# The first steps of a convolution kernel in another order: two transforms interleaved, eleven input blocks held, one product folded into the sum

## The chip, the cores and the metric

The kernel runs on one core of a Trainium2 chip. The metric is the device time of one execution in microseconds (us). Before the change it is 835.12 us, the median of three runs (835.08, 835.12 and 838.7).

The engines are named as the profile names them: PE (TensorE, matmuls), PEld (its weight loads), DVE (VectorE), ACT (ScalarE), POOL (GpSimd), and SP, whose queue starts nearly all DMAs.

## The reference

```python
def _attn_ref(x, h):                     # x (8, 6336, 128), h (6336, 128)
    L = 2 * S
    Xf = np.fft.rfft(x, n=L, axis=1)
    Hf = np.fft.rfft(h, n=L, axis=0)
    return np.fft.irfft(Xf * Hf[None, :, :], n=L, axis=1)[:, :S, :]

def _moe_ref(x, w_gate, w1, w2, capacity):        # capacity 128, on the result above
    scores = np.einsum('bsd,d->bs', x, w_gate)
    out = x.copy()
    for b in range(B):
        top_idx = np.argpartition(-scores[b], capacity)[:capacity]
        xe = x[b, top_idx]
        ye = np.maximum(xe @ w1, 0.0) @ w2
        g = 1.0 / (1.0 + np.exp(-scores[b, top_idx]))
        out[b, top_idx] = x[b, top_idx] + g[:, None] * ye
    return out
```

A causal convolution of every batch with h over 6336 positions, done by transforms, and then an expert on the 128 best rows of each batch. Everything is float32.

## The kernel before, in words

The length is split as 50 x 128 (n1 by n2), so a transform has two steps of matmuls. Eight units of work carry the input x (units 0 to 7); unit -1 is h itself. Steps of a unit:

- **a**: the products over n1. A unit has eight input blocks (q = 0 to 7) of 512 KB. A block is loaded (`load_x`, L112 to L117), folded by a sum and a difference of its halves (`fold`, L119 to L122, 128x512 each), and multiplied in two steps t = 0, 1 of 16 matmuls (`products_a`, L166 to L181; the trace shows 32 matmuls a step). The results leave PSUM by copies (`leave_a`, L183 to L197).
- **h**: the products of h over n2, in 13 chunks of four k (the last has two), `stage_h` L214 to L244: matmuls into a ring of four PSUM banks, two turned products on ACT and the cosine product in place (L229, L230), then `join` on DVE, which adds the two (L237) and has the spectrum written twice to DRAM as `hd` (L241).
- **b**: the products of a unit of x over n2, 13 chunks, `stage_b` L246 to L273: matmuls (L251), two products with the spectrum on DVE (L268, one in place in `reg` or `big`, one into a buffer `tx`), and a sum and a difference of them on POOL (L273). `tx` and `st` come from one ring of five buffers (`wide`). The matrix of a chunk (`tab_wb`) and its spectrum are loaded to the six slots of `wbuf`.
- **c**, **d**: back over n2 and n1 (L286, L303), and then the scores, the search for the best rows and the experts. The change does not touch them.

A list named `plan` holds all steps in program order; each engine and SP's queue runs its instructions in that order, and `merge` (L633) interleaves two lists evenly. For the first steps the list is: all of a(-1), all of a(0), then 13 steps "j", then all of a(1). Step j of chunk c has the h products of chunk c+1 and the b products of unit 0 of chunk c, with the spectrum taken from SBUF. From then on c of a unit is merged with b of the next, and a with d. Six blocks are held at first; the load of a later block waits until the block whose slot it takes has been used. Of the folds those of blocks 0 to 15, 21 and 23 are DVE's, the others POOL's.

Of the kernel before, what the change touches and what calls it, by code (L numbers as in the profile page):

```python
# [33 lines left out]
def conv_moe(ctx, tc, x, h, w_gate, w1, w2, fa_d, wb_d, wc_d, at_d, tri_d, cst_d, out):  # L34
# [26 lines left out]
    hring = banks + [spare]  # L61

# [41 lines left out]
    def place(n):  # L104
# [4 lines left out]
        i = 10 + max(0, q - 4) % 3 if u >= 2 else 3 + n % 6 if n < 16 else n - 13  # L109
# [104 lines left out]
    def stage_h(c, wt):  # L214
# [6 lines left out]
        for k in range(0, kn, 2):  # L221
            pt = turn(hring)
            for i in range(2):
                nc.tensor.matmul(pt[:, i * 256:i * 256 + 256], wt[:, k + i], rows_of(-1, k0 + k + i),  # L224
                                 start=True, stop=True)
            pv = pt.rearrange("p (a r d) -> p a r d", r=2, d=HD)
            tv = turned[:, k * 256:k * 256 + 512].rearrange("p (a r d) -> p a r d", r=2, d=HD)
# [415 lines left out]
    plan = merge(a_list(-1), a_list(0)[:0]) + merge(a_list(0), [])  # L643
    plan += [("j", -1, c) for c in range(len(KCH))] + merge(a_list(1), [])
# [13 lines left out]
    users = [s for s in plan if s[0] in "bdj"]  # L658
# [6 lines left out]
    def ask(used):  # L665
        while asked[0] < len(users):
# [4 lines left out]
            if sum(1 if o[0] == "j" else 0 if o in own else 3 if o[0] == "b" and o[1] >= SINGLE else 2  # L671
# [23 lines left out]
    for n in range(6):  # L695
        load_x(n)
# [18 lines left out]
    for s in plan:  # L715
        kind, unit = s[0], s[1]
        n = (unit + 1) * 8
        if kind in "bdj":
            ask(used)
            used += 1  # L720
        if kind == "a":
            q, t = s[2:]
            if unit < 2 and t == 0:
                fold_to(min(n + q + 4, 15) if unit < 1 else 23)
# [7 lines left out]
            if t and n + q < 10:  # L732
                load_x(n + q + 6)
# [179 lines left out]
```

## Time and profile before

| | us |
|---|---|
| median of three runs | 835.12 |
| the profiled execution | 838.41 |
| its span in the trace | 836.6 |
| PE busy | 756.0 (90%) |
| DVE busy | 653.6 (78%) |
| POOL busy | 547.3 (65%) |
| ACT busy | 383.6 (46%) |
| chain that ended last: PE 69%, DVE 19%, issue 6%, DMA 4% | |

The profiled execution took 1.8 us more than its span, and 3.3 us more than the median of the runs. Busy time is an average over stages with different limits, so the first stages have to be read apart. The granted clock of TensorE is given as a share of full speed: 1.00 is 2.4 GHz, 0.50 is 1.2 GHz.

### The profile page before, as it was taken

What the parts mean: (1) busy time and instruction counts of PE and PEld (TensorE: products, weight loads), DVE (VectorE), ACT (ScalarE), POOL (GpSimd) and SP (SyncE); (2) the same over time, 40 slices, a digit from 0 to 9 for tenths busy, and PEclk for the clock granted to TensorE, in tenths of its full rate; (3) what the DMA queues carried; (4) which work ended last, traced back from release to release, by engine and by line L of the source; (5) the groups of instructions that cost most, each with busy time, mean ns of one, the idle gap of its engine ahead of it and who ended that gap; (6) DMA issues with size and microseconds to landing.
All of it is one profiled execution on the core that took longest, in us unless ns stands there. A gap on an engine that the chain in (4) does not pass through costs nothing.

```text
span 836.6 us, 36709 instructions
## 1 busy us (share of the span) xinstructions
PE 756.0 (90%) x16189; PEld 676.5 (81%) x16189; DVE 653.6 (78%) x1103; ACT 383.6 (46%) x625; POOL 547.3 (65%) x387
## 2 busy tenths in 40 slices
PE   6699899999999999999999999899999997689733
PEld 6688788898889888898888888788897887578733
DVE  6459846756576798999778998899689989876882
ACT  5587543464346334543464346433653343233340
POOL 0029929966987699679866896569865566125531
PEclk9899899999999999999999999999999999889966
DMA  8639536468737864777377646796678455204400
GB/s 296 212 133 346 171 121 221 146 213 251 272 109 230 260 228 125 229 246 257 107 228 246 209 151 199 252 322 206 202 232 256 132 165 174 83 10 133 136 11 9
DMA packets 82135, 157.45 MB, mean 188 GB/s; under 512 B 9350, under 2 KB 30072, under 8 KB 81976
## 3 DMA queue, kind: packets, MB, share of 16 engines
q1 hardware_dynamic: 81080, 154.05, 57.1%
q8 instruction: 127, 2.08, 1.0%
q0 software_dynamic: 896, 1.05, 0.5%
q14 instruction: 32, 0.26, 0.1%
HBM read 121.77 MB, written 33.29 MB: 185 GB/s over the span
## 4 chain that ended last, share of the span: by engine, by line
PE 69%; DVE 19%; issue 6%; DMA 4%; POOL 1%; SPq 0%; ACT 0%; POOLq 0%; DVEq 0%; ACTq 0%
PE pb L286 23%; PE pt L251 18%; PE pb L303 11%; PE pt L180 10%; DVE cmp L418 3%; PE pb L180 2%; PE pb L570 2%; DVE num L420 2%; DVE tx L268 2%; DMA out<-st 1%; DVE ss L319 1%; PE pb L224 1%; DVE reg L262 1%; DMA big<-tab_wb 1%; DVE st L307 1%
## 5 line engine op out<-in xcount | busy, mean ns | idle before, releaser
L287 ACT COPY half<-pb 114x512 f32<-114x512 f32 x224 | 147.3, 658 | 248.2 <-PE pb L286 247.4
L314 POOL TENSOR_TENSOR tm<-st,wg 114x1024 f32<-114x1024 f32 x63 | 151.0, 2399 | 80.3 <-DVE st L308 49.5
L273 POOL TENSOR_TENSOR big<-big,tx 128x512 f32<-128x512 f32 (+1 forms) x104 | 131.5, 1297 | 77.2 <-DVE tx L268 65.3
L273 POOL TENSOR_TENSOR reg<-reg,tx 128x512 f32<-128x512 f32 (+1 forms) x104 | 130.7, 1290 | 53.4 <-DVE tx L268 29.7
L286 PEld LDWEIGHTS pb<-wc,reg 128*50 128x50 f32 x4096 | 121.0, 129 | 12.2 <-issue 8.9
L286 PEld LDWEIGHTS pb<-wc,big 128*50 128x50 f32 x4096 | 118.3, 127 | 14.8 <-issue 13.2
L286 PE MATMUL pb<-wc,reg 128*50 128x64 f32 x4096 | 125.8, 223 | 1.4 <-DVE st L308 1.4
L286 PE MATMUL pb<-wc,big 128*50 128x64 f32 x4096 | 122.6, 221 | 0.0
L303 PE MATMUL pb<-half,wbuf 114*50 114x128 f32 x1792 | 110.4, 273 | 7.3 <-DVE st L308 5.1
L303 PEld LDWEIGHTS pb<-half,wbuf 114*50 114x50 f32 x1792 | 95.7, 122 | 17.5 <-DVE st L308 5.9
L251 PE MATMUL pt<-big,wbuf 128*128 128x256 f32 x352 | 88.0, 396 | 0.0
L251 PE MATMUL pt<-reg,wbuf 128*128 128x256 f32 x352 | 87.7, 397 | 0.0
L307 DVE TENSOR_TENSOR st<-pb,st 114x512 f32<-114x512 f32 x64 | 44.1, 688 | 55.6 <-PE pb L303 42.1
L268 DVE TENSOR_TENSOR tx<-pt,wbuf 128x1024 f32<-128x1024 f32 (+1 forms) x65 | 76.3, 1174 | 0.0
L251 PEld LDWEIGHTS pt<-big,wbuf 128*128 128x128 f32 x352 | 64.4, 188 | 14.4 <-DVE tx L268 0.5
L251 PEld LDWEIGHTS pt<-reg,wbuf 128*128 128x128 f32 x352 | 63.9, 188 | 14.0
L197 ACT COPY reg<-pt 128x800 f32<-128x800 f32 x66 | 58.0, 929 | 33.8 <-PE pt L180 32.2
L268 DVE TENSOR_TENSOR reg<-pt,wbuf 128x1024 f32<-128x1024 f32 (+1 forms) x39 | 45.9, 1177 | 24.3 <-PE pt L251 24.3
L197 ACT COPY big<-pt 128x800 f32<-128x800 f32 x59 | 51.6, 929 | 22.9 <-PE pt L180 22.9
L322 DVE TENSOR_REDUCE ss<-tm 114x16 f32<-114x1024 f32 x48 | 58.4, 1216 | 2.3 <-POOL tm L314 1.7
L180 PE MATMUL pt<-fa,big 50*64 50x100 f32 x2336 | 59.1, 249 | 0.2 <-issue 0.2
L180 PEld LDWEIGHTS pt<-fa,big 50*64 50x64 f32 x2336 | 51.8, 133 | 6.3 <-issue 3.7
(159 smaller groups left out, 1118.1 us busy)
## 6 DMA issues: line engine op xcount, KB each, us to landing
wbuf<-tab_at SPq DMA_DIRECT2D x128, 200.0 KB
out<-st SPq DMA_DIRECT2D x128, 200.0 KB
wbuf<-tab_wb SPq DMA_DIRECT2D x84, 256.0 KB
wbuf<-hd SPq DMA_DIRECT2D x84, 256.0 KB
big<-in_x SPq DMA_DIRECT2D x37, 512.0 KB
half<-in_x SPq DMA_DIRECT2D x15, 512.0 KB
hd<-st SPq DMA_DIRECT2D x24, 256.0 KB
reg<-in_x SPq DMA_DIRECT2D x12, 512.0 KB
```

The costliest lines, as they stand in the source:

```text
L180: nc.tensor.matmul(o, w, tab[lanes, c], start=True, stop=True)
L197: nc.scalar.copy(out=o, in_=i)
L251: nc.tensor.matmul(pt[:, k * 256:k * 256 + 256], wt[:, k], rows_of(unit, k0 + k), start=True, stop=True)
L268: v.tensor_tensor(out=dst.rearrange("p h a j k t -> p k h a j t"), in0=src, in1=w, op=ALU.mult)
L273: g.tensor_tensor(out=yv[:, :, r], in0=yv[:, :, r], in1=zv[:, :, 1 - r], op=ALU.add if r else ALU.subtract)
L286: nc.tensor.matmul(pt[i2 * 64:i2 * 64 + N1, o:o + HD], w, wc[:, i2], start=True, stop=True)
L287: nc.scalar.copy(out=hv[0:LN, c * 4 + j:c * 4 + j + 2].rearrange("p j r m t -> p (j r) t m"), in_=pt[0:LN].rearrange("p (j t m) -> p j t m ...
L303: nc.tensor.matmul(pt[r][a * 64:a * 64 + N1, c * 128:c * 128 + 128], ats[c // 2][0:LN, c % 2, a, r], hv[0:LN, :, r, m], start=True, stop=True)
L307: v.tensor_tensor(out=st[:, 0:512], in0=pt[1][0:LN], in1=st[:, 512:1024], op=ALU.add)
L314: e.tensor_tensor(out=tm.rearrange("p (a d) -> p a d", d=n), in0=st.rearrange("p (a d) -> p a d", d=n), in1=w.unsqueeze(1).broadcast_to([L ...
L322: v.tensor_reduce(out=ss[u][:, :, :, 4 * i:4 * i + 4].rearrange("p b s c -> p s c b"), in_=tm.rearrange("p (s c b d) -> p s c b d", s=2, c ...
L418: v.tensor_tensor(out=cv, in0=cur.unsqueeze(2).broadcast_to([LN, nb, nv, HD]), in1=nth[:, :, 0:nv].unsqueeze(3).broadcast_to([LN, nb, nv, ...
```

## The change

The list of first steps becomes: all of a(-1); the 13 h steps merged with all of a(0); the 13 b steps of unit 0 merged with the first five blocks of a(1); the last three blocks of a(1). With it:

- the step "j" is gone. Unit 0 now gets its matrix and its spectrum by `load_b` as the later units do, so `tab_wb` is loaded a second time and `hd` is read back for it; a join is put one chunk after its h step.
- eleven blocks are held (slots 2 to 12) in place of six, and eight blocks of h and three of x are asked for before the first step.
- POOL folds blocks 9, 11, 13, 15 and 16 to 23; DVE folds 0 to 8, 10, 12 and 14.
- the results of a(0) leave by ACT for t = 0 and by DVE for t = 1; five half banks of a(-1) leave by DVE; a(1) uses four single banks (`fringe`) and leaves by ACT.
- ACT no longer multiplies by the cosine: `join` does it in one SCALAR_TENSOR_TENSOR with the sum.

```diff
+    fringe = [(banks[0], banks[1], None), (banks[2], spare, None)]
...
-        i = 10 + max(0, q - 4) % 3 if u >= 2 else 3 + n % 6 if n < 16 else n - 13
+        i = 10 + max(0, q - 4) % 3 if u >= 2 else 2 + n % 11
...
-        if unit < 2:
+        if unit == -1:
             pt = turn(wheel)
+        elif unit == 1:
+            pt = turn(fringe)
...
-        if unit == 1 and q > 2:
-            engines = "sv" if pt[2] is None else "v" if pt[2] is pairs[0] else "s"
+        if unit == -1 and pt[2] is None and q % 3:
+            engines = "sv"
+        if unit == 0 and t:
+            engines = "v"
...
-            nc.scalar.mul(out=pt, in_=pt, mul=cst[:, 2:3])
...
-                v.tensor_tensor(out=sv[:, k:k + 2], in0=got[k // 2].rearrange("p (k a d) -> p k a d", a=4, d=HD),
+                v.scalar_tensor_tensor(out=sv[:, :, k:k + 2], in0=got[k // 2].rearrange("p (a k d) -> p a k d", a=4, d=HD),
+                                       scalar=cst[:, 2:3], op0=ALU.mult, op1=ALU.add,
...
-    plan = merge(a_list(-1), a_list(0)[:0]) + merge(a_list(0), [])
-    plan += [("j", -1, c) for c in range(len(KCH))] + merge(a_list(1), [])
+    chunks = range(len(KCH))
+    plan = merge(a_list(-1), []) + merge([[("h", -1, c)] for c in chunks], a_list(0))
+    plan += merge([[("b", 0, c)] for c in chunks], a_list(1)[0:5]) + merge(a_list(1)[5:], [])
...
-    for n in range(6):
+    for n in range(8):
+        load_x(n)
+    nc.sync.dma_start(out=cst, in_=cst_d)
+    nc.sync.dma_start(out=fa, in_=fa_d[:, 0])
+    for n in range(8, 11):
         load_x(n)
...
-            fold(done[0], v if done[0] < 16 or done[0] in (21, 23) else g)
+            fold(done[0], v if done[0] < 8 or done[0] < 16 and done[0] % 2 == 0 else g)
...
-                fold_to(min(n + q + 4, 15) if unit < 1 else 23)
+                fold_to(min(n + q + 4, 23))
...
-            if t and n + q < 10:
-                load_x(n + q + 6)
+            if t and n + q < 13:
+                load_x(n + q + 11)
...
+        elif kind == "h":
+            spectra.append(stage_h(s[2], tabs.pop(s)[0]))
+            if s[2]:
+                spectra.pop(0)()
+        elif kind == "b":
+            if spectra:
+                spectra.pop(0)()
```

PE after the first unit, before: the last step of a(0) (L180, two banks of `pt`), and then h (L224) and b (L251) by turns.

```order
L180 MATMUL pt_69<-fa,half 64x2x50 x16
L224 MATMUL pb_70<-reg_75,wbuf 128x256 x2
L224 MATMUL pb_71<-reg_75,wbuf 128x256 x2
L224 MATMUL pb_72<-reg_75,wbuf 128x256 x2
L224 MATMUL pm<-reg_75,wbuf 128x256 x2
L251 MATMUL pt_68<-big,wbuf 128x256 x4
```

PE at the same stage now (L183 is a, L229 is h):

```order
L229 MATMUL pb_72<-reg_75,wbuf 128x4x64 x2
L229 MATMUL pm<-reg_75,wbuf 128x4x64 x2
L183 MATMUL pt_68<-fa,big 64x2x50 x16
L183 MATMUL pt_69<-fa,big 64x2x50 x16
L229 MATMUL pb_70<-reg_75,wbuf 128x4x64 x2
L229 MATMUL pb_71<-reg_75,wbuf 128x4x64 x2
```

The steps of a(0) now stand between h chunks, and no b stands there.

DVE in a(-1), before, from the fold of block 6 on, with the waits (L121 and L122 are the two halves of a fold):

```order
L121 TENSOR_TENSOR half<-half 128x512 [waits DMAHW7_49,PE_49]
L122 TENSOR_TENSOR half<-half 128x8x64 [waits DVE_49,PE_49]
L121 TENSOR_TENSOR half<-half 128x512 [waits DMAHW0_49,PE_49]
L122 TENSOR_TENSOR half<-half 128x8x64 [waits DVE_49,PE_49]
L121 TENSOR_TENSOR half<-half 128x512 [waits DMAHW1_49,PE_49]
```

DVE now, from the fold of block 7 on (L122 and L123 are the fold, L198 the copy of a half bank, `big` holds the first blocks of x):

```order
L122 TENSOR_TENSOR half<-half 128x512
L123 TENSOR_TENSOR half<-half 128x8x64
L122 TENSOR_TENSOR big<-big 128x512
L123 TENSOR_TENSOR big<-big 128x8x64
L198 COPY reg_75<-pb_71 128x2x200 x2
L122 TENSOR_TENSOR big<-big 128x512
L123 TENSOR_TENSOR big<-big 128x8x64
L198 COPY reg_75<-pb_71 128x2x200
```

Copies that PE's ring of PSUM buffers waits for now stand behind folds that do not wait for PE.

POOL from its first b chunk on, before (L273 is b, L121 and L122 a fold):

```order
L273 TENSOR_TENSOR big<-big,tx 128x2x32x8 x6
L121 TENSOR_TENSOR half<-half 128x512
L122 TENSOR_TENSOR half<-half 128x8x64
L273 TENSOR_TENSOR big<-big,tx 128x2x32x8 x4
L121 TENSOR_TENSOR half<-half 128x512
```

POOL now, from the fold of block 19 and the first b chunk on (L276 is b):

```order
L122 TENSOR_TENSOR big<-big 128x512
L123 TENSOR_TENSOR big<-big 128x8x64
L276 TENSOR_TENSOR big<-big,tx 128x2x32x8 x2
L122 TENSOR_TENSOR big<-big 128x512
L123 TENSOR_TENSOR big<-big 128x8x64
L276 TENSOR_TENSOR big<-big,tx 128x2x32x8 x4
L122 TENSOR_TENSOR big<-big 128x512
```

Between the first and the last of its 13 b chunks POOL has four folds, both before (blocks 16 to 19) and now (20 to 23); eight others stand ahead of the first chunk now.

## Rows read from the trace of the kernel before

**Rows 1.** Stages; columns: window, us, busy (instructions) by engine, PEclk, DMA share, GB/s
```profile
0.00:24.20 24.20, 15.22 (x525) 14.38 (x528) 15.19 (x24) 13.81 (x21) 0.20 (x4) 1.00 0.87 292
24.20:46.03 21.83, 16.82 (x509) 16.11 (x500) 6.50 (x10) 13.84 (x22) 0.00 (x0) 0.77 0.48 163
46.03:95.66 49.63, 46.51 (x203) 37.10 (x200) 44.13 (x52) 37.33 (x77) 37.91 (x31) 1.00 0.75 261
95.66:112.96 17.30, 15.53 (x512) 14.82 (x513) 11.10 (x12) 9.80 (x15) 10.08 (x8) 0.80 0.11 38
112.96:836.60 723.64, 661.91 (x14454) 594.07 (x14453) 576.70 (x1006) 308.81 (x492) 499.12 (x345) 0.97 0.58 184
```

**Rows 2.** Chain of waits, pieces in order of time: start us, us, what
```profile
20.72 2.31 issue
23.43 1.37 PE pt L180 x64
...
36.38 2.52 issue
...
57.26 1.82 PE pt L251 x8
59.07 1.83 PE pb L224 x8
```

**Rows 3.** DVE, timeline: start us, us, engine, line, op [idle before]
```profile
5.10 0.69 DVE L121 TENSOR_TENSOR half<-half 128x512 f32<-128x512 f32 x1 [4.10 <-DMA half<-in_h]
...
6.44 0.69 DVE L121 TENSOR_TENSOR half<-half 128x512 f32<-128x512 f32 x1
```

**Rows 4.** DVE, groups by line: busy us, mean ns | idle before
```profile
L237 DVE TENSOR_TENSOR st<-pb,half 128x512 f32<-128x512 f32 x19 | 12.5, 682 | 13.7 <-ACT pb L230 13.7
L195 DVE COPY reg<-pt 128x800 f32<-128x800 f32 x3 | 3.0, 993 | 0.3
L195 DVE COPY reg<-pb 128x400 f32<-128x400 f32 x4 | 2.3, 576 | 5.9 <-PE pb L180 5.9
L485 DVE SCALAR_TENSOR_TENSOR work<-pm,work 114x256 bf16<-114x256 f32 x6 | 2.3, 418 | 0.1
```

**Rows 5.** Timeline where DVE and POOL fold together
```profile
99.90 1.72 POOL L121 TENSOR_TENSOR half<-half 128x512 f32<-128x512 f32 x1
...
100.52 1.65 DVE L122 TENSOR_TENSOR big<-big 128x512 f32<-128x512 f32 x1
```

**Rows 6.** DVE, timeline: the two products of the first b chunk
```profile
51.80 1.23 DVE L268 TENSOR_TENSOR big<-pt,st 128x1024 f32<-128x1024 f32 x1 [0.84 <-PE pt L251]
52.95 1.21 DVE L268 TENSOR_TENSOR tx<-pt,st 128x1024 f32<-128x1024 f32 x1
```

**Rows 7.** POOL, timeline: its first b chunk, a fold, two later chunks
```profile
54.34 2.50 POOL L273 TENSOR_TENSOR big<-big,tx 128x512 f32<-128x512 f32 x2 [53.89 <-DVE tx L268]
...
64.09 1.28 POOL L121 TENSOR_TENSOR half<-half 128x512 f32<-128x512 f32 x1
...
66.69 4.98 POOL L273 TENSOR_TENSOR big<-big,tx 128x512 f32<-128x512 f32 x4
```

**Rows 8.** Issues of DMAs up to 114 us: count, KB each
```profile
half<-in_h SPq DMA_DIRECT2D x8, 512.0 KB
hd<-st SPq DMA_DIRECT2D x24, 256.0 KB
wbuf<-tab_wb SPq DMA_DIRECT2D x15, 256.0 KB
```

**Rows 9.** Two stretches with the DMA engines full, columns as in rows 1
```profile
5.00:12.00 7.00, 6.01 (x146) 5.71 (x150) 6.72 (x11) 2.80 (x5) 0.00 (x0) 1.00 1.01 373
60.00:80.00 20.00, 19.97 (x87) 16.10 (x87) 19.58 (x25) 15.95 (x33) 18.56 (x16) 1.00 0.98 343
```

**Rows 10.** PE, timeline: the first matmuls of a(1), with the wait ahead of them
```profile
95.66 1.01 PE L180 MATMUL pb<-fa,half 50*64 50x100 f32 x32 [3.07 <-DVE st L237]
```

**Rows 11.** The stretch from there on, columns as in rows 1
```profile
95.66:104.00 8.34, 7.96 (x208) 7.77 (x212) 6.38 (x6) 4.61 (x8) 8.26 (x7) 0.59 0.22 75
```

More of the change, by code (lines that the diff above doesn't have):

```diff
@@ L223, in stage_h @@
             for i in range(2):
[L224 to L227, printed above, removed]
+                nc.tensor.matmul(pt.rearrange("p (a i j t) -> p i a j t", i=2, j=32, t=2)[:, i], wt[:, k + i],
+                                 rows_of(-1, k0 + k + i).rearrange("p (a j) t -> p a j t", a=4), start=True, stop=True)
+            pv = pt.rearrange("p (u r x) -> p u r x", r=2, u=2)
+            tv = turned[:, k * 256:k * 256 + 512].rearrange("p (u r x) -> p u r x", r=2, u=2)
             for r in range(2):
                 nc.scalar.mul(out=tv[:, :, 1 - r], in_=pv[:, :, r], mul=cst[:, 3 + r:4 + r])
-            nc.scalar.mul(out=pt, in_=pt, mul=cst[:, 2:3])
             got.append(pt)
@@ L656, in conv_moe @@
             plan += merge(d_list(u), []) + [("end", u)]
-    users = [s for s in plan if s[0] in "bdj"]
+    users = [s for s in plan if s[0] in "bdh"]
     tabs = {}
@@ L670, in ask @@
                 break
-            if sum(1 if o[0] == "j" else 0 if o in own else 3 if o[0] == "b" and o[1] >= SINGLE else 2
+            if sum(1 if o[0] == "h" else 0 if o in own else 3 if o[0] == "b" and o[1] >= SINGLE else 2
                    for o in users[used:asked[0] + 1]) > 6:
@@ L717, in conv_moe @@
         n = (unit + 1) * 8
-        if kind in "bdj":
+        if kind in "bdh":
             ask(used)
@@ L731, in conv_moe @@
                 fold(n + 6, g)
-            if t and n + q < 10:
-                load_x(n + q + 6)
-            if t and (unit, q) == (-1, 3):
-                nc.sync.dma_start(out=cst, in_=cst_d)
-                nc.sync.dma_start(out=fa, in_=fa_d[:, 0])
-            if t and (unit, q) == (0, 3):
+            if t and n + q < 13:
+                load_x(n + q + 11)
+            if t and (unit, q) == (-1, 1):
                 ask(0)
@@ L740, in conv_moe @@
                 load_x(n + 7)
-            if unit == 0 and q == 0 and t:
+            if unit == 0 and q == 5 and t:
                 load_constants()
@@ L744, in conv_moe @@
                 visit("pqx" if q and q % 2 == 0 else "x")
-        elif kind == "j":
-            c = s[2]
-            if c == 6:
+        elif kind == "h":
[5 more added lines that the diff above has]
+                spectra.pop(0)()
+            if (unit, s[2]) == (0, 4):
                 v.tensor_copy(out=upper16[0:LN], in_=upper)
@@ L750, in conv_moe @@
                 v.tensor_scalar(out=lanes16[:, 1:2], in0=cst[:, 0:1], scalar1=-1.0, scalar2=None, op0=ALU.mult)
-            if c == 0:
-                spectra.append(stage_h(0, tabs[s][0])())
-            join = stage_h(c + 1, tabs["j", -1, c + 1][0]) if c + 1 < len(KCH) else None
-            n = KCH[c][1] * HD
-            st = spectra.pop()
-            stage_b(0, c, (tabs.pop(s)[0], [st[:, 0:n], st[:, n:2 * n]]))
-            if join:
-                spectra.append(join())
-            if s[2] < 8:
-                load_x(16 + s[2])
-            if s[2] in (2, 4, 6, 8):
-                fold_to(15 + s[2] // 2)
-        elif kind == "b":
             stage_b(*s[1:], tabs.pop(s))
```

6 lines of the change are left out of this document (2 added, 4 removed).

## The prediction

> **What bounds the kernel now.** I read the windows by stage first. In [rows 1] the steps stand in a row: a(-1) to 24.2 us, a(0) to 46.0, the thirteen "j" steps to 95.7, a(1) to 113.0, and from there on c with b, which the change does not touch. The reader is to see that PE is not the same bound in each: in a(0) it is busy 16.8 of 21.8 us at a mean granted clock of 0.77, and in a(1) 15.5 of 17.3 us at 0.80, while the DMA engines are all but idle in a(1) (share 0.11) and POOL's first instruction of these stages ends a wait of 53.9 us [rows 7]. Everything after 113.0 us is taken as it is, 723.6 us. So the question is only when PE can begin c(0), and in what state.
>
> The chain of waits gives the prices of PE's work at full clock [rows 2]: a pair of a-steps (64 matmuls) 1.37 us, a chunk of b 1.82, a chunk of h 1.83. A unit of a is then 8 x 1.37 = 11.0 us, the 12.5 chunks of h or of b 22.9 us each. The three units of a, h and b are 78.7 us of PE. They can begin behind the first half of a fold (5.1 + 0.7, rows 3), so without a wait c(0) would start at 84.5. The 28.5 us above that are stalls, low clock, and j steps in which DVE and POOL are nearly full (44.1 and 37.9 of 49.6 us, rows 1).
>
> **a(-1).** All h blocks are now asked for at once, so no load waits for a slot. DVE becomes the pace: it folds 8 h blocks and blocks 0 and 2 of x at 1.34 us each (6.44 - 5.10, [rows 3]), and makes five half-bank copies of 0.576 us [rows 4]: 13.4 + 2.9 from 5.1 on, 21.4 us. Each copy stands behind a fold in DVE's queue, and PE's next use of that bank waits for it; once DVE waits in turn for PE's step and the signals (0.9). Folds 0 and 2 of x run beside POOL's first folds, and there an instruction of DVE took 1.65 us beside a POOL fold of 1.72 [rows 5] instead of 0.69: four of them could lose 3.8 us, none nothing; I take 1.0, since PE's waits let part of it pass. With PE's last step (half of 1.37) and its copy out of PSUM (1.0, as the 0.993 of rows 4), h starts at about 25.0. Bounds: 22.3 with the contention and the last step hidden, 27.3 with one stall of PE's sequencer as at 20.72 (2.31 us, rows 2). That is where a(0) starts today: this part gains nothing.
>
> On these folds the Trainium skill (SBUF — State Buffer, Who interferes with whom) says that a DVE instruction with two SBUF inputs and a POOL instruction that reads SBUF exclude each other for a whole instruction. By it each of the four would wait up to the 1.28 us of a POOL fold, 5.1 us in all; the measured 1.65 is a loss of 0.96, so the trace bears out the sign and not the whole size.
>
> **h beside a(0).** 12.5 x 1.83 + 8 x 1.37 = 33.9 us of PE, if it is never waited for: 59 us. DVE's part is 25 joins, 8 copies of 0.993 and two folds. The join's new form is not in the trace at this shape; the nearest row is 0.418 us for 256 elements [rows 4], twice that is 0.84, the plain sum is 0.682 for 512. By 0.68 DVE has 27.7 us, by 0.84 31.6, both under 33.9; cost nothing, and if that cover goes, 25 x 0.16 = 4 us at most. ACT loses a product and has half the copies. So the a(0) products that took 21.8 us alone come to 11.0, and the j steps lose their h half.
>
> **b beside a(1), the new bound.** POOL cannot begin b before the first chunk of unit 0 has passed PE and DVE. That chunk needs its two tables, which stand in SP's queue behind all earlier DMAs. By [rows 8] a block is 0.524 MB, a matrix and a write of `hd` 0.262: 24 blocks 12.6, 13 matrices 3.3, the joins of eight chunks written twice 4.2, small tables 0.5, its own two 0.5; together 21.1 MB. The first 11.7 MB (19 blocks, 6 matrices) go at the 373 GB/s of the full stretch of blocks, the other 9.4 at the 343 of the mixed one [rows 9]: 2 + 31.4 + 27.4 = 60.8 us. PE is ready at 59, so the queue of DMAs decides by 2 us. With 1.8 on PE and two products of 1.23 and 1.21 on DVE [rows 6] POOL starts at 65.2.
>
> From there POOL has 24 instructions of 1.25 (4.98 for four, rows 7) and two halves, 31.3 us, and four folds (blocks 20 to 23) of 2.6 (66.69 - 64.09, [rows 7]), 10.4. The tables of chunk 2 are 3.1 MB later, at 69.8, so its products are ready at 74.1, when POOL has been idle 1.3 us. End of POOL's b: 65.2 + 31.3 + 10.4 + 1.3 = 108.2 us. PE has only 34 us of work in this stretch, DVE 30; both hide under POOL. PE's last step of a(1) needs the fold of block 23, which stands ahead of POOL's last 4.5 chunks, so PE is done near 98 and waits some 10 us.
>
> That wait has a price. In [rows 10] PE waited 3.07 us, and in the 8.34 us behind it [rows 11] the granted clock was 0.59 on average, so at its lower level (0.50) for four fifths of it: 8.34 x 0.41 = 3.4 us of PE lost. Today c(0) starts with no such wait. Bounds: 0, since a wait of 2.31 us at 20.72 was followed by a pair at full speed (1.37 us, rows 2), and 3.4; by the length of the wait I take 3.4.
>
> **The sum.** c(0) at 108.2 + 3.4 = 111.6 in effect, against 112.96: 1.4 us earlier. The profiled execution took 838.41 us (span 836.6 and 1.8 around it), so 837.0. It lies 3.3 us above the median of the runs, and nothing in one trace says where; I take the same off: **833.7 us**. With the clock kept it is 830.3; with h at 27.3 and 4 us lost to the joins the b stage starts 4.4 later, 838.1. The forecast's own range is 830 to 838.
>
> **Rivals.**
>
> *Faster: a(-1) ends at DVE's pace and c(0) keeps its clock.* h at 22.3, done by 56.2; the queue at 373 GB/s throughout has the first tables at 2 + 56.6 = 58.6; POOL from 63.0 to 104.7, no idle time, full clock: 8.3 us gained, 830.1 and less 3.3, 826.9. For it: blocks alone moved at 373; one wait of 2.31 us cost no clock. Against: half of the bytes are writes and small tables at 343, and PE's wait is 10 us. With the clock lost it would be 830.3.
>
> *No change: the DMA queue is the bound of all of it.* 6.5 MB are added (matrices and spectra for unit 0). At 343 GB/s from the first block on, chunk 2 has its tables at 2 + 70.6 = 72.6, DVE is done with it at 76.9, and POOL with 10.5 chunks (26.3) and three folds (7.8) behind it at 111.0; with the clock 114.4, 1.4 later than before: 836.5. For it: a share of 0.98 over 20 us at that rate. Against: the 373 of the first stretch.
>
> *Slower: the stalls of a(0) come along into the h stage.* Today a(0) takes 21.8 us for 11.0 of products; the 10.8 are stalls in which PE waits for nothing the profile shows (2.52 us at 36.38, rows 2, and others like it) and low clock behind them. If these stay with the full DMA queues, h ends at 69.8, POOL runs from 74.2 to 115.9, and c(0) is at 119.3 with the clock: 6.4 later, 841.5. It decides from some 8 us of loss on. Against it: the a-steps give PE 64 matmuls in 1.37 us, and the stalls stand in stretches of these alone; in the j steps PE had 203 in 49.6 us (rows 1), with the DMA engines at 0.98 for 20 of them (rows 9), and was busy for 46.5 of them. Mixed with h it is some 610 matmuls in 34 us, nearer to the latter. The Trainium skill (Runtime: NRT & Kernel Launch, Instruction fetch mechanics) has instructions fetched in blocks of 256 with the crossing mostly hidden; by it this rival would hardly exist, but today's 2.31 and 2.52 us are not hidden.
>
> **How the numbers follow.** Forecast 0.40, faster rival 0.33, no change 0.14, slower 0.13. About 0.5% (4.2 us) is what a measurement here can tell from no change, so faster means under 830.9. Of the forecast's 0.40 some 0.07 lies there: faster 0.40, same 0.47, slower 0.13. The range runs from under the faster rival, 824, to the slower one's 841.
>
> **What would show it.** Right: h (L229) starts near 25, the first b (L254) near 61 behind a table's DMA, POOL (L276, L122) without a gap from 65 to 108, PE idle some 10 us ahead of L289, and a granted clock near 0.5 behind it. Wrong: L289 before 105 or after 113; PE, not POOL, ending last in b; stalls of 2 us and more between L229 and L183; POOL's chunk not at 2.5 us.

## The result, and the profile after

The changed kernel takes 842.34 us (median of 14 runs, 838.85 to 845.78), the kernel before 835.5 us in the same comparison (14 runs). The ratio is 1.0079, 95% interval 1.0058 to 1.0100: slower by 0.8%, where 833.7 us was forecast. The profiled execution took 845.78 us (span 844.0), 7.4 us more than that of before.

The windows by stage (columns as in [rows 1]) are, in order: a(-1); h beside a(0); b of unit 0 beside a(1); the rest from c(0) on.

```profile
0.00:29.99 29.99, 18.33 (x513) 17.14 (x513) 19.04 (x28) 13.42 (x17) 7.29 (x9) 0.88 0.95 362
29.99:69.92 39.93, 39.88 (x612) 31.30 (x613) 25.18 (x34) 27.23 (x57) 14.20 (x12) 0.92 0.85 293
69.92:116.05 46.13, 38.62 (x617) 30.02 (x617) 31.97 (x32) 15.20 (x34) 41.14 (x34) 0.99 0.64 202
116.05:844.00 727.95, 666.48 (x14449) 598.17 (x14449) 576.05 (x1005) 307.33 (x492) 498.74 (x345) 0.96 0.57 182
```

c(0) starts at 116.05 us, 3.1 later than in [rows 1], and all behind it takes 4.3 us more (727.95 against 723.64), although the change does not touch it. In the h stage PE is full (39.88 of 39.93 us); in the b stage POOL is (41.14 of 46.13), and PE has 7.5 us to spare.

PE's timeline shows where the time goes. The columns are those of [rows 10]; "issue" is a wait for nothing that the profile shows.

```profile
14.45 0.82 PE L183 MATMUL pb<-half 50*64 50x100 f32 x26 [1.70 <-DVE reg L198]
...
21.18 0.30 PE L183 MATMUL pt<-half 50*64 50x100 f32 x2 [0.82 <-issue]
...
27.10 0.43 PE L183 MATMUL pb<-half 50*64 50x100 f32 x2 [2.94 <-issue]
...
29.99 3.78 PE L229 MATMUL pb<-reg,wbuf 128*128 128x256 f32 x8 [0.96 <-ACT reg L200]
33.70 2.78 PE L183 MATMUL pt<-fa,big 50*64 50x100 f32 x64
36.41 1.20 PE L229 MATMUL pb<-reg,wbuf 128*128 128x256 f32 x4
...
38.45 1.60 PE L183 MATMUL pt<-fa,big 50*64 50x100 f32 x64
39.98 3.02 PE L229 MATMUL pb<-reg,wbuf 128*128 128x256 f32 x12
...
115.37 0.46 PE L289 MATMUL pb<-wc,big 128*50 128x64 f32 x4 [4.64 <-POOL big L276]
116.05 6.26 PE L289 MATMUL pb<-wc,big 128*50 128x64 f32 x124 [0.22 <-POOL big L276]
```

h starts at 29.99, behind 3.76 us of stalls without a cause in the profile and 1.70 us for a copy of DVE. Its first chunk takes 3.78 us and the first pair 2.78, twice the prices of [rows 2]; later on, from start to start, a pair takes 1.53 (38.45 to 39.98) and a chunk behind a pair 2.04 (36.41 to 38.45). At the end PE waits 4.64 us for POOL, and the first piece of c(0) takes 6.26 us. The granted clock (seventh number, before the DMA share) says why these pieces are long:

```profile
10.00:15.00 5.00, 3.30 (x94) 3.11 (x90) 4.30 (x8) 2.31 (x3) 0.00 (x0) 1.00 1.04 411
15.00:20.00 5.00, 5.00 (x168) 5.00 (x161) 4.90 (x8) 3.03 (x5) 0.77 (x1) 0.66 1.02 407
20.00:25.00 5.00, 3.33 (x145) 2.94 (x134) 2.71 (x4) 4.08 (x6) 4.80 (x4) 1.00 1.05 393
25.00:30.00 5.00, 1.94 (x36) 1.63 (x36) 2.75 (x4) 0.95 (x2) 1.52 (x1) 0.59 1.02 406
30.00:35.00 5.00, 5.00 (x40) 3.77 (x44) 0.58 (x1) 1.68 (x4) 4.84 (x5) 0.50 0.51 193
...
115.00:120.00 5.00, 4.41 (x78) 4.21 (x80) 0.00 (x0) 1.04 (x2) 0.99 (x2) 0.50 0.00 0
```

It is at its lower level (0.50, 1.2 GHz) at the start of h, behind the stall of 2.94 us, and again at the start of c(0), behind the wait of 4.64. The DMA engines are full (share 1.02 to 1.05) from 10 to 30 us; in [rows 9] they were so at 5 to 12, and from 10 to 25 us before the change their share was 0.74 to 0.99.

POOL's timeline, against [rows 7]: its first chunk of b, then a fold (two instructions, L122 and L123) for each of blocks 20 to 23 between the chunks.

```profile
74.54 2.51 POOL L276 TENSOR_TENSOR big<-big,tx 128x512 f32<-128x512 f32 x2 [29.88 <-DVE tx L271]
77.01 1.29 POOL L122 TENSOR_TENSOR big<-big 128x512 f32<-128x512 f32 x1
...
104.72 11.27 POOL L276 TENSOR_TENSOR big<-big,tx 128x512 f32<-128x512 f32 x10
```

From 74.54 to 115.99 POOL has no gap: 41.5 us. Ahead of it, it is idle for 29.9 us. The join has its own row in the groups of DVE, 742 ns, between the 682 and the 840 of the estimate [rows 4]:

```profile
L241 DVE SCALAR_TENSOR_TENSOR st<-pb,cst,half 128x512 f32<-128x512 f32 x19 | 13.4, 742 | 0.0
```

### The profile page after: what moved, and what is told of

It is laid out like the page before. It is cut to its first block, busy times and chain, and to the rows that moved or that the text cites. A ratio compares the mean times of both kernels' runs of the same rounds, so it can differ in the third digit from the quotient of the medians.

```text
span 844.0 us, 36752 instructions
## 1 busy us (share of the span) xinstructions
PE 763.3 (90%) x16189; PEld 676.6 (80%) x16189; DVE 652.2 (77%) x1097; ACT 363.2 (43%) x599; POOL 561.4 (67%) x399
## 3 DMA queue, kind: packets, MB, share of 16 engines
q8 instruction: 127, 2.08, 1.0%
q0 software_dynamic: 896, 1.05, 0.4%
## 4 chain that ended last, share of the span: by engine, by line
PE 71%; DVE 18%; issue 4%; DMA 3%; POOL 3%; SPq 0%; ACT 0%; POOLq 0%; DVEq 0%; ACTq 0%
PE pb L289 24%; PE pt L254 18%; PE pb L306 11%; PE pt L183 10%; DVE cmp L421 3%; PE pb L229 2%; POOL big L276 2%; DVE num L423 2%; PE pb L573 2%; DVE reg L265 1%; DVE tx L265 1%; DVE ss L322 1%; PE pb L183 1%; DVE ss L325 1%; DVE st L310 1%
## 5 line engine op out<-in xcount | busy, mean ns | idle before, releaser
L276 POOL TENSOR_TENSOR reg<-reg,tx 128x512 f32<-128x512 f32 (+1 forms) x104 | 130.6, 1288 | 49.9 <-DVE tx L271 26.0
L276 POOL TENSOR_TENSOR big<-big,tx 128x512 f32<-128x512 f32 (+1 forms) x104 | 130.5, 1288 | 49.9 <-DVE tx L271 38.9
L289 PEld LDWEIGHTS pb<-wc,big 128*50 128x50 f32 x4096 | 122.6, 131 | 19.3 <-issue 12.6
L289 PE MATMUL pb<-wc,big 128*50 128x64 f32 x4096 | 127.2, 225 | 4.9 <-POOL big L276 4.9
L271 DVE TENSOR_TENSOR tx<-pt,wbuf 128x1024 f32<-128x1024 f32 (+1 forms) x78 | 91.6, 1174 | 0.0
L200 ACT COPY reg<-pt 128x800 f32<-128x800 f32 x59 | 51.6, 928 | 36.8 <-PE pt L183 36.8
L271 DVE TENSOR_TENSOR big<-pt,wbuf 128x1024 f32<-128x1024 f32 (+1 forms) x39 | 46.0, 1179 | 25.0 <-PE pt L254 24.8
L183 PE MATMUL pt<-fa,big 50*64 50x100 f32 x2496 | 64.1, 252 | 0.4 <-issue 0.4
L183 PEld LDWEIGHTS pt<-fa,big 50*64 50x64 f32 x2496 | 56.3, 135 | 8.0 <-issue 3.9
```

The source lines that it names most:

```text
L183: nc.tensor.matmul(o, w, tab[lanes, c], start=True, stop=True)
L200: nc.scalar.copy(out=o, in_=i)
L271: v.tensor_tensor(out=dst.rearrange("p h a j k t -> p k h a j t"), in0=src, in1=w, op=ALU.mult)
L276: g.tensor_tensor(out=yv[:, :, r], in0=yv[:, :, r], in1=zv[:, :, 1 - r], op=ALU.add if r else ALU.subtract)
L289: nc.tensor.matmul(pt[i2 * 64:i2 * 64 + N1, o:o + HD], w, wc[:, i2], start=True, stop=True)
```

## The experiments

Times are medians, with the ratio to the kernel before, run on the same chip, and its 95% interval. Executions of one kernel differ by up to 11 us here, so a profile, which is one execution, gives the places, and the runs the verdict. Where two experiments are compared, their intervals say whether the runs part them.

**1. The folds of POOL ahead of b.** The changed kernel with the folds of blocks 16 to 23 asked for early:

```diff
-                fold_to(min(n + q + 4, 23))
+                fold_to(min(n + q + 4, 15) if n + q < 12 else min(2 * q + 9, 23) if unit == 0 else 23)
```

> The changed kernel with one thing moved: POOL's folds of blocks 20 to 23 stand ahead of its first b chunk, in the 30 us in which POOL had nothing to do (44.7 to 74.5), in place of between the b chunks. Theory A (POOL sets the end of the b stage, and its wait costs c(0) its clock): POOL's 13 chunks end 10.4 us earlier, near 106, PE becomes the last at about 107.5, c(0) starts there without a wait and at full clock: 8.5 + 3.8 us less, near 830 to 832 in the median, faster than the kernel before. Rival B (the tables and spectra read back from DRAM pace the b chunks): c(0) stays near 114 to 116 and the time near 842.

835.21 us (12 runs), 1.0003 [0.9981, 1.0026]: 7 us under the changed kernel, no different from before. The windows of the h and the b stage, and PE's rows behind them:

```profile
28.27:66.75 38.48, 38.42 (x613) 30.07 (x613) 26.37 (x34) 27.28 (x57) 25.84 (x20) 0.96 0.88 309
66.75:107.47 40.72, 37.90 (x612) 29.81 (x612) 31.14 (x32) 14.27 (x33) 31.23 (x26) 1.00 0.71 226
```

```profile
73.95 2.05 PE L254 MATMUL pt<-big,wbuf 128*128 128x256 f32 x8 [1.54 <-DMA wbuf<-tab_wb]
...
107.47 3.82 PE L289 MATMUL pb<-wc,big 128*50 128x64 f32 x128
```

POOL has 31.23 us left in b, c(0) starts at 107.47 without a wait and at the full clock (3.82 us, where 6.26 stood). So POOL, with four folds between its chunks, set the end of b in the change. The tables of b did not: they cost 1.54 us. Of the 8.6 us by which c(0) came earlier in this execution, 5.4 are the b stage (40.72 for 46.13) and 3.2 stood ahead of it, 1.7 of them in a(-1), whose steps the edit does not touch. c(0) came where it was expected, the expected 830 to 832 us did not come: they were worked out from a profiled execution 3.4 us above the change's median.

**2. The wait kept, PE kept busy in it.** The changed kernel with 11 matmuls whose result nobody uses, between a(1) and c(0):

```diff
+            if (unit, q, t) == (1, 7, 1):
+                for i in range(11):
+                    nc.tensor.matmul(pairs[1][:, 0:256], ident, tri.rearrange("p a b -> p (a b)"),
+                                     start=True, stop=True)
```

> The changed kernel with eleven matmuls more, whose results nobody uses, on PE between a(1) and c(0): about 5 us of PE work in the wait for POOL. Theory A (the wait lets the clock fall, and 3.8 us are lost behind it): c(0) starts at the same time, 116, at full clock, and the whole is 3 to 4 us shorter, near 838.5. Rival C (in the first c and b steps something else is the bound, so the clock costs nothing there): no change, 842.

838.18 us (12 runs), 1.0045 [1.0017, 1.0073], 4.2 under the changed kernel; the two intervals overlap a little, so the size is rough. c(0) starts as late, but at full speed:

```profile
111.28 4.91 PE L740 MATMUL pt<-tri 128*128 128x256 f32 x22 [0.99 <-issue]
116.12 3.78 PE L289 MATMUL pb<-wc,big 128*50 128x64 f32 x128
```

What the wait costs beyond itself is the clock behind it. The stage from c(0) on takes 720.3 us here (span 836.4). In the three traces with a wait of over 4 us ahead of it, it took 726.9 to 727.95 (the change, experiments 3 and 12). In the others it took 721.4 to 724.7, but for experiment 10 with 727, which has no such wait: one trace can be that long for other reasons, so this bears the reading out and does not prove it.

**3. All copies of a(-1) on ACT** (the rule that gave five of them to DVE is taken out):

```diff
-        if unit == -1 and pt[2] is None and q % 3:
-            engines = "sv"
```

> The changed kernel with all copies of a(-1) on ACT, as before the change. Theory D (the five copies that stand behind folds in DVE's queue hold PE back and so make h start at 30 us): h starts near 27.5, the b stage and c(0) move with it, 2 to 3 us less, near 839.5. Rival E (landing of the blocks and PE's own stalls of 0.8 and 2.9 us set that start): h stays at 29 to 31, and ACT's extra 2.4 us may add up to 2: 842 to 844.

842.85 us (6 runs), 1.0082 [1.0051, 1.0114]: no different from the change. PE no longer waited for DVE in a(-1), but its stalls without a cause were 1.08, 3.61 and 1.59 us, 6.3 in all for 3.76, and h started at 29.91. The copies behind DVE's folds are not what makes a(-1) long.

**4. The cosine in the sum alone**, put into the kernel before (`stage_h` of the change, nothing else).

> The kernel before with the cosine product taken into the join, and nothing else of the change. Theory: ACT is off the path in the j steps, and DVE, which is on it from the sixth step on, pays about 0.06 us more for each of 25 joins (0.74 against 0.68): 0 to 1.5 us more, 835.5 to 837. Rival: the join waited for the cosine product, and without it the j steps are shorter: 2 to 4 us less.

837.31 us (12 runs), 1.0007 [0.9979, 1.0035]: no difference, as expected. The join takes 742 ns here too.

**5. The ring of eleven blocks alone**, in the kernel before:

```diff
-        i = 10 + max(0, q - 4) % 3 if u >= 2 else 3 + n % 6 if n < 16 else n - 13
+        i = 10 + max(0, q - 4) % 3 if u >= 2 else 2 + n % 11
...
-    for n in range(6):
+    for n in range(8):
+        load_x(n)
+    nc.sync.dma_start(out=cst, in_=cst_d)
+    nc.sync.dma_start(out=fa, in_=fa_d[:, 0])
+    for n in range(8, 11):
         load_x(n)
...
-            if t and n + q < 10:
-                load_x(n + q + 6)
-            if t and (unit, q) == (-1, 3):
-                nc.sync.dma_start(out=cst, in_=cst_d)
-                nc.sync.dma_start(out=fa, in_=fa_d[:, 0])
+            if t and n + q < 13:
+                load_x(n + q + 11)
...
-            if s[2] < 8:
-                load_x(16 + s[2])
```

> The kernel before with the ring of eleven blocks alone: blocks 0 to 10 asked for at the start, block n + 11 behind step n, none in the j steps; order, folds and copies as before. Theory Q (the full DMA queue slows a(-1): the h blocks land later beside the others, and PE's stalls without a named cause grow): a(0) starts 2 to 4 us later than the 24.2 of before, at 26 to 28, with DMA engines at a share over 1.0 in 10 to 25 us; c(0) at 113 to 116, 836 to 839 us. Rival F (the copies and folds of DVE and POOL in the new split made a(-1) longer, not the queue): a(0) starts at 24.2 plus or minus 0.7, and the time is that of before or under it, 833 to 835.5.

840.96 us (5 runs), 1.0063 [1.0038, 1.0088]. Only the loads are changed (those of two small tables, `cst` and `fa`, come earlier with the blocks), POOL folds nothing and DVE copies nothing in a(-1), and DVE folds ahead of PE without a wait from 8.5 us on. Yet a(0) starts at 29.00, 5.06 us later than in before and later than the 26 to 28 expected:

```profile
14.56 0.99 PE L180 MATMUL pt<-half 50*64 50x100 f32 x34 [0.56 <-issue]
...
21.29 0.31 PE L180 MATMUL pt<-half 50*64 50x100 f32 x3 [3.61 <-issue]
...
27.29 0.61 PE L180 MATMUL pb<-half 50*64 50x100 f32 x8 [1.50 <-issue]
...
29.00 1.56 PE L180 MATMUL pt<-fa,big 50*64 50x100 f32 x32
```

```profile
10.00:15.00 5.00, 4.44 (x150) 4.25 (x146) 4.86 (x8) 3.58 (x6) 0.00 (x0) 1.00 1.03 406
15.00:20.00 5.00, 2.68 (x118) 2.48 (x110) 4.86 (x9) 3.34 (x5) 0.00 (x0) 1.00 1.03 414
20.00:25.00 5.00, 3.71 (x116) 3.72 (x120) 4.69 (x8) 2.83 (x5) 0.00 (x0) 0.75 1.01 379
25.00:30.00 5.00, 3.50 (x82) 3.19 (x78) 2.38 (x4) 2.36 (x4) 0.00 (x0) 0.50 0.42 137
```

The stalls add up to 5.67 us (0.68 and 2.31, 2.99 in all, in before), the DMA engines are full while they last, and the clock falls behind them. So the loads asked for ahead are enough by themselves for the late start of h.

**6 and 7. Six blocks first, the rest later.** Experiment 1 with a ring of six; 7 has also a pair of a(1) behind chunks 0, 1, 3, 5, 7 and 9 of b, and the five small tables later. Of the edit, the order of the later loads:

```diff
...
-            if t and n + q < 13:
-                load_x(n + q + 11)
+            if t and unit < 1:
+                for k in ((n + q + 6,) if n + q < 8 else ((14, 16), (15, 17), (18,), (19,), (20, 21), (22,), (23,), ())[q]):
+                    load_x(k)
...
```

> Experiment 1 (all folds of POOL ahead of b) with the blocks asked for later: six at the start, one more behind each step of a(-1), the last ten spread over a(0), so that 14 blocks and not 19 are asked for by the end of a(-1). Theory Q: h starts at 24.5 to 26.5 (28.27 in experiment 1) and its first chunk takes under 2.5 us (3.42 there), since PE stalls less ahead of it; the bytes are the same in all, so the first tables of b come at 65 to 69 and part of the gain is given back; c(0) at 104 to 107 (107.5 there), 831 to 835 us. Rival F: h starts at 28 plus or minus 0.7 as in experiment 1, later blocks make POOL's folds and the tables later, c(0) at 108 or more, 836 and over.

> As experiment 6, with a pair of a(1) behind chunks 0, 1, 3, 5, 7 and 9 of b (six and not five beside b, two alone at the end) and the five small tables asked for behind the first pair of a(1), not in a(0). In experiment 1 PE waited 1.54 us for the tables of chunk 2, and three pairs at the end took 1.87 us each, at the pace of ACT's copies. If PE's order is the bound of b: c(0) 1 to 2 us earlier than in experiment 6 and 830 to 834 us. Rival (POOL's chunks, 31.3 us from its first one on, are the bound there): c(0) within 0.7 us of experiment 6, with PE waiting for POOL ahead of it, and a low granted clock behind.

841.88 us (12 runs), 1.0064 [1.0036, 1.0091], and 839.44 (12 runs), 1.0038 [1.0014, 1.0063]. Both theories missed: h started at 32.07 and 30.49. The reason is another wait, which I had built in myself; DVE's and PE's timelines of experiment 6:

```profile
23.23 0.69 DVE L122 TENSOR_TENSOR half<-half 128x512 f32<-128x512 f32 x1 [5.43 <-DMA half<-in_x]
...
25.19 1.43 PE L183 MATMUL pb<-half 50*64 50x100 f32 x26 [3.42 <-DVE reg L198]
...
32.07 2.08 PE L229 MATMUL pb<-reg,wbuf 128*128 128x256 f32 x8 [1.00 <-ACT reg L200]
```

A fold of x waits 5.43 us for its block, a copy of a(-1) stands behind it in DVE's queue, and PE waits for the copy. In b the tables came late as well (waits of 2.39 and 2.09 us in 6; 1.49, 0.79 and 2.80 in 7). Experiment 7 can't tell PE's order from POOL for that reason: c(0) came at 114.92.

**8 and 9. The loads paced.** Experiment 1 with the h blocks first, and block n + 8 in the slot that step n of a(-1) frees; 9 has also all copies of a(-1) on ACT.

```diff
-        i = 10 + max(0, q - 4) % 3 if u >= 2 else 2 + n % 11
+        i = 10 + max(0, q - 4) % 3 if u >= 2 else 2 + n % 8 if n < 16 else (10, 11, 12, 2, 3, 4, 5, 6)[n - 16]
...
-    for n in range(8, 11):
-        load_x(n)
...
-            if t and n + q < 13:
-                load_x(n + q + 11)
+            if t and unit < 1:
+                for k in (8 + q,) if unit < 0 else (16 + 2 * q, 17 + 2 * q) if q < 2 else (18 + q,) if q < 6 else ():
+                    load_x(k)
...
-            if t and (unit, q) == (-1, 1):
+            if t and (unit, q) == (-1, 4):
                 ask(0)
```

> Experiment 1 with the loads paced by their slots: the eight h blocks at the start, then one block behind each step of a(-1) in the slot which that step has freed, the first six matrices behind step 4 of a(-1) and not behind step 1, blocks 16 to 23 behind the steps of a(0). By the end of a(-1) 16 blocks are asked for, not 19, and no fold of DVE stands before a block that is asked for late. Theory Q (DMA engines at a share over 1.0 hold up PE's instructions): share in 10 to 25 us under 0.9, PE's stalls of a(-1) without a named cause under 3 us in all, h at 24.5 to 26.5 (28.27 in experiment 1), its first chunk under 2.5 us; some 1.5 MB move into the h stage, 4 us of the queue, so the tables of b cost part of the gain; c(0) at 104 to 107.5; 831 to 835 us. Rival T (the tables are the bound all the same, the bytes up to them do not change): h earlier, but the first chunks of b wait 4 us and more for their tables, c(0) at 107 to 110; 835 to 838. Rival F: the stalls stay, h at 28 and later, 836 and over.

> As experiment 8, with all copies of a(-1) on ACT, none on DVE. In experiment 1 PE waited 1.33 and 0.47 us for two copies of DVE that stood behind folds. If these waits decide once the queue is not full: h 0.7 to 1.8 us earlier than in experiment 8, and c(0) with it unless the tables of b are the bound. If not: h within 0.5 us of experiment 8, the time within 1 us of it.

835.28 us, 0.9991 [0.9961, 1.0021], and 836.53, 1.0006 [0.9979, 1.0033] (12 runs each). In 8 the share was 0.69 and 0.84 in 15 to 25 us, PE had no stall over 0.5 us in a(-1), and h started at 26.49 with a first chunk of 2.08 us. The time is that of experiment 1 all the same. In 9, with PE waiting less for DVE, the loads came faster, the share was 0.99 and 1.01, the stalls 0.64, 1.96 and 3.70 us, and h started at 29.17: what was won at DVE was lost at the stalls. The gain in 8 was given back: PE's first chunk of b came 2.89 us earlier than in experiment 1 (63.86 for 66.75) and c(0) only 0.49 (106.98). PE and SP's queue:

```profile
73.29 2.05 PE L254 MATMUL pt<-big,wbuf 128*128 128x256 f32 x8 [3.06 <-DMA wbuf<-tab_wb]
```

```profile
65.83 2.08 SPq L245 DMA_DIRECT2D hd<-st  x4
68.00 0.59 SPq L145 DMA_DIRECT2D wbuf<-tab_wb  x1
```

The matrix that PE waited for was issued at 68.00, behind four writes of the spectrum.

**10 and 11. A quiet DMA queue in a(-1).** The kernel before with the first six x blocks asked for behind the last step of a(-1); in 11 a small DMA of what that step wrote stands ahead of them.

> The kernel before with a quiet DMA queue in the second half of a(-1): only the eight h blocks are asked for there, the first six x blocks behind its last step, their folds behind that. a(0) must start later and the whole is slower; what counts is a(-1) alone, PE's stalls without a named cause from 14 us on (0.68 and 2.31 us before, 0.56, 3.61 and 1.50 in experiment 5). Theory Q (they come with full DMA engines): no stall over 0.5 us there once the share falls, and PE through with a(-1) by 21 to 22.5 us (24.2 before). Rival I (they come with the count of instructions, however full the queue): stalls of 2 to 4 us in all between 14 and 24 us, and a(-1) done at 23.5 or later.

> Experiment 10 again, with the six x blocks really held back: SP waits ahead of them for a small DMA (2 columns) that reads what the last step of a(-1) wrote, so the DMA queue is empty from the last h block's landing, about 13 us, to the end of a(-1). Only a(-1) counts, the whole is slower. Theory Q: no stall of PE without a named cause over 0.5 us between 14 us and its end, a(-1) done by 20 to 22.5 us. Rival I (the count of instructions alone): 2 to 4.5 us of such stalls there as in experiment 10 (1.52 and 2.87), done at 23.5 or later.

One execution each; only a(-1) counts (840.52 and 842.11 us in all). Experiment 10 failed as a test: the slots were free early, SP issued the blocks from 12.67 us on, the share stayed at 0.90 and 0.86 in 10 to 20 us, and the stalls were 1.52 and 2.87. In 11 the loads were held:

```profile
15.00:20.00 5.00, 4.78 (x205) 4.43 (x198) 1.59 (x3) 5.00 (x9) 0.00 (x0) 1.00 0.08 25
20.00:25.00 5.00, 1.34 (x51) 0.95 (x43) 0.00 (x0) 2.68 (x5) 0.00 (x0) 1.00 0.03 3
```

```profile
17.28 0.31 PE L180 MATMUL pt<-half 50*64 50x100 f32 x3 [0.22 <-issue]
...
21.50 0.40 PE L180 MATMUL pb<-half 50*64 50x100 f32 x8 [1.25 <-issue]
```

With a share of 0.08 and 0.03 the same two stalls are 0.22 and 1.25 us, and a(-1) is through by 22.6 (24.1 in before). So each theory holds in part: 1.5 us of stalls are there with idle DMA engines, and more with busy ones: 3.0 in before, 4.4 and 5.7 in experiments 10 and 5. Each of these is one execution.

**12. The change, paced.** The changed kernel with the loads of experiment 8, the folds left in b.

> The changed kernel with the loads paced as in experiment 8 and nothing else changed: POOL's four folds stand in b as in the change. If the late start of h is the mis-sized term of the prediction (29.99 us, forecast 25.0) and POOL's 41.5 us from its first chunk on set the end: h at 26 to 28, POOL's first chunk 2 to 4 us before its 74.54, c(0) 2 to 4 us before 116.05, still with a wait for POOL of 2 us and more ahead of it and a low granted clock behind; 837.5 to 840.5 us, 2 to 5 under the changed kernel's 842.34. Rival T (the tables of b come no earlier, since the same bytes stand ahead of them): POOL's first chunk within 1 us of 74.54, and 841 to 844 us.

839.57 us (12 runs), 1.0061 [1.0035, 1.0087], 2.8 under the change; the intervals overlap, so that the runs alone do not show a gain. h started at 25.11, POOL's first chunk stood at 68.23 (74.54 in the change), its last ended at 109.7, and the wait was still there:

```profile
109.05 0.46 PE L289 MATMUL pb<-wc,big 128*50 128x64 f32 x4 [4.66 <-POOL big L276]
109.72 5.61 PE L289 MATMUL pb<-wc,big 128*50 128x64 f32 x124 [0.22 <-POOL big L276]
```

The end of b moves with POOL's first chunk one for one, 6.3 us, at POOL's 41.5 us (68.23 to 109.7), and that chunk with the start of h (4.9 us earlier) and the clock there (1.00 in 25 to 30 us). So the tables do not hold it. This is one execution, and it moved more than expected; the runs gained less, and how many of them start h so early can't be told from one trace.

**13 and 14. The tables of b ahead.** Experiment 8 with the tables of chunk 2 asked for ahead of the last two joins' writes; 13 has also the five small tables behind the first pair of a(1).

```diff
             spectra.append(stage_h(s[2], tabs.pop(s)[0]))
+            if s[2] == 12:
+                ask(used)
             if s[2]:
                 spectra.pop(0)()
```

> Experiment 8 with the tables of chunk 2 of b asked for ahead of the last two joins' writes in SP's queue, and the five small tables behind the first pair of a(1). In experiment 8 they were issued at 68.00 us, behind four writes that waited for DVE from 65.83, while their slots had been free from 63.9; PE waited 3.06 us for them at 70.2. If SP's order is what gives the gain back: that wait goes under 1 us, c(0) at 104 to 106 (106.98), 832 to 835 us. Rival B (the DMA engines are full from 30 to 70 us and only swap what they move): the wait stays at 2 us and more, or moves to another chunk, c(0) within 1 us of experiment 8, 834 to 837. Rival P (POOL, 31.3 us from its first chunk on, is the bound): the wait goes, and POOL's last chunk still ends at 106 to 107.

> Experiment 8 with the tables of chunk 2 of b asked for ahead of the last two joins' writes, and the five small tables left in a(0), as in experiment 8. In experiment 13 their five issues, 70.27 to 72.80 us, stood ahead of the tables of chunk 3, for which PE waited 3.51 us. If SP's order is what costs: no wait of PE over 1.5 us for a table in 60 to 85 us, POOL's first chunk to its last under 34.5 us, c(0) 41 us or less behind PE's first chunk of b (43.1 in experiment 8, 42.9 in 13), 831 to 834 us, faster than before. Rival B (full DMA engines): a wait of 2 us or more for another table, the time that of experiments 8 and 13, 833.5 to 836.

833.84 us, 0.9975 [0.9947, 1.0004], and **831.81 us, 0.9946 [0.9917, 0.9976]** (12 runs each). In 13 the wait for chunk 2 was gone, but PE waited 3.51 us for chunk 3, whose tables stood behind the small ones, and c(0) came at 110.09. Its steps of a(-1) are those of 8, 12 and 14, but in this execution PE stalled in them:

```profile
19.41 0.30 PE L183 MATMUL pt<-half 50*64 50x100 f32 x2 [1.44 <-issue]
...
24.78 0.30 PE L183 MATMUL pb<-half 50*64 50x100 f32 x2 [2.40 <-issue]
```

In 14 PE's and SP's rows answer to those of experiment 8, and the windows are the h and the b stage:

```profile
70.91 2.05 PE L254 MATMUL pt<-big,wbuf 128*128 128x256 f32 x8 [0.86 <-DMA wbuf<-tab_wb]
...
104.68 3.79 PE L289 MATMUL pb<-wc,big 128*50 128x64 f32 x128 [0.22 <-POOL big L276]
```

```profile
65.91 0.42 SPq L145 DMA_DIRECT2D wbuf<-tab_wb  x1
```

```profile
26.66:63.76 37.10, 37.05 (x612) 29.09 (x613) 25.95 (x35) 27.26 (x57) 26.21 (x20) 1.00 1.00 371
63.76:104.50 40.74, 38.11 (x612) 30.00 (x613) 31.15 (x32) 14.33 (x33) 31.37 (x26) 1.00 0.75 239
```

The matrix is issued at 65.91, PE waits 0.86 us in place of 3.06, and c(0) is at 104.68, 40.9 us behind the first chunk of b (43.1 in experiment 8). This version is faster than both kernels: by 0.5% than the one before. Its interval still overlaps that of experiment 8 ([0.9961, 1.0021]), so the share of the order in that gain is read from the places.

## Why the prediction was wrong, step by step

**The step that failed: when h starts.** The prediction had 25.0 us for it, with DVE as the pace of a(-1) and one stall of PE as the upper bound, 27.3; it came at 29.99. DVE was not the pace: its last two copies of a(-1) waited for PE.

```profile
22.29 0.58 DVE L198 COPY reg<-pb 128x400 f32<-128x400 f32 x1 [2.25 <-PE pb L183]
...
27.73 0.58 DVE L198 COPY reg<-pb 128x400 f32<-128x400 f32 x1 [2.22 <-PE pb L183]
```

All asked-for blocks were booked as a gain ("no load waits for a slot"). Their cost was not: full DMA engines from 10 to 30 us, 3.76 us of stalls where 2.99 had stood, and a mean clock of 0.66 in 15 to 20 us and of 0.59 in 25 to 30. Experiment 5 shows this with the loads alone. Asking later takes part of it back: h starts at 25.11 to 26.99 in the four traces with the paced a(-1) (experiments 8, 12, 13 and 14), and at 28.27 to 30.25 in the three with that of the change (the change, experiments 1 and 2). The 1.70 us for a copy of DVE is real, but where it was taken out (3 and 9) the stalls grew by more, to 6.3 us.

**What the stalls are.** The rows that would have told it were there. [rows 2] has the stalls of 2.31 and 2.52 us, and [rows 9] the full DMA engines; I took the stalls as a property of the a-steps and never asked what they depend on. The Trainium skill (Runtime: NRT & Kernel Launch, Instruction fetch mechanics) has the crossing to the next block of instructions mostly hidden. The traces show that these stalls are that crossing, and that it is not hidden here. The page of before counts, for 16189 matmuls and as many weight loads, 127 packets of 16 KB of the kind "instruction", one for every 255 of them:

```profile
q8 instruction: 127, 2.08, 1.0%
```

Between each two of PE's five stalls from 17.03 to 38.90 us in before lie 126 matmuls. And by the packets' own times in the 16 traces, each of the 29 "issue" stalls over 0.15 us in a(-1) ends 1.2 to 1.5 us behind the landing of such a packet: in before it moved from 20.69 to 21.65 us and PE went on at 23.03; in the change from 24.71 to 25.82, and PE went on at 27.10. A later packet makes a longer stall: in experiment 11, with idle DMA engines, one started 1.57 us behind the crossing before it, and the stall was 1.25 us; in experiment 5, with full ones, 4.13 and 3.61. In the a-steps such a crossing comes every 2.7 us of PE's work at full clock, in the h stage of the change some 8 us apart (612 matmuls and as many loads in 39.93 us).

**The h stage, 33.9 us forecast, 39.93 measured.** Experiment 14 has it at a clock of 1.00 throughout: 37.10. So 2.8 us are the clock behind the late stall, and 3.2 are a term that the sum lacked: each change from a chunk to a pair and back. A pair is 1.53 us from start to start beside 1.37 [rows 2], a chunk behind it 2.04 beside 1.83. Eight rounds of 0.16 and 0.21 make 3.0.

**The tables of b.** The DMA queue was to decide by 2 us. It did not in the change, since PE came at 69.92 and not at 59. Where PE came earlier (8, 13), the tables were late, but less by bytes than by order: experiment 14 moves only their place in SP's queue, and 2.2 of the 3.06 us go.

**POOL in b.** 31.3 + 10.4 = 41.7 us were forecast, 41.5 measured; the 1.3 us of idle time did not come. 108.2 plus the 9.3 by which POOL began late (74.54 for 65.2, where the prediction's own terms make 65.0), less 1.3 and 0.2, is the 116.0 of the trace. This mechanism was right, and it is the worst part of the change: experiment 1 moves only the place of the folds, and its runs are 7 us shorter. That POOL is idle ahead of b, here for 29.9 us, follows from the order of the work; the prediction booked the four folds in b without asking why they stood there.

**The wait and its clock.** 10 us of wait were forecast, 4.64 came, since PE was late itself. The price, 3.4 us, had the right size: from the rows the first pieces of c and b lost 2.5 (from c(0) to the second c, 10.03 us for 7.57), and experiment 2 gets some 4.2 back. That 2.31 us of wait had cost no clock in [rows 2] was a poor lower bound: the place mattered as much as the length.

**The join and ACT's product.** 0.742 us, hidden under PE, worth nothing either way (experiment 4).

**The rivals.** The slower one had the right time, 841.5, by the wrong place. It put the stalls into the h stage; there is none over 0.5 us between 30 and 70 us in the change (experiment 12 has one of 1.03), and the argument against it (more work for each instruction) held. The stalls grew in a(-1), for which the prediction had at most one of them. Forecast and rivals alike had h start between 22.3 and 27.3, so the case that came was in none of them; 842.3 lies just above the range's 841, into which the slower rival's own 841.5 does not fit either.

**What stays open.** What decides how late the packet of instructions comes. Counted from the crossing before it, it started 2.3 to 4.1 us later in a(-1) of experiment 5 (share 1.00 to 1.03 in between), and 0.4 us later or less at 16 to 22 us in 8 and 14, where the DMA engines were less full; but in a(0) of experiments 10 and 11 it could take 4.5 and 4.7 us at a share of 0.44 and 0.52. So a full queue is not all of it. PE's own pace counts too: in 8 and 14 there was no stall over 0.5 us, with a share of 0.69 to 0.84 from 15 to 25 us, but PE had waited 2.5 us for DVE just before and ran at half the clock in 15 to 20 us, so that the packets may have come in meanwhile; in 13, the same steps with a wait of 1.0 us and the full clock, the share was 0.93 and 0.96 and the stalls 1.44 and 2.40. No run parts the two.

## What to carry to other kernels

Loads that are asked for as early as there is room are not free: here PE's own instructions came later behind them, so let the slots pace them. Count PE's instructions as well as its work: where small matmuls follow each other without a wait, the next packet of instructions can be what PE waits for, and a stall without a named cause can be held against the packets' times. An engine that will be the bound of the next stage should have its other work done in the stage before, above all if it is idle there. Price a change of order by the two kinds of work run by turns, not by each in a row of its own.

## What the runs showed of the hardware

- PE's stalls without a named cause in a(-1) ended 1.2 to 1.5 us behind the landing of a 16 KB packet of instructions, 29 of 29 in the 16 traces; one such packet came for every 255 matmuls and weight loads.
- In the 16 steps of a(-1) these stalls were 1.5 us in all with nearly idle DMA engines (share 0.08 and 0.03 in 15 to 25 us, experiment 11), 3.0 and 4.4 with 0.65 to 0.99 (before, experiment 10), 3.8 with 0.93 and 0.96 (experiment 13), and 3.2 to 6.3 with 0.99 to 1.05 (the change, experiments 1, 5 and 9). In experiments 8, 12 and 14 they were 0.2 or less with 0.69 to 0.89, where PE had waited 1.6 to 2.5 us for DVE and run at half the clock for a part of the time.
- Matmuls of two shapes by turns cost more than each in a row: 64 small ones 1.53 for 1.37 us, eight large ones behind them 2.04 for 1.83.
- A wait of 4.6 us cost PE some 2.5 us more behind it, at the lower clock; with eleven matmuls for nothing in the wait, the first piece behind it took 3.78 us in place of 6.26.
